# Loads of a decode kernel: from two half-loads on SyncE's and GpSimd's queues to whole loads on SyncE's

## The chip, the cores and the metric

The kernel runs on one core of one Trainium2 chip. The metric is the time of one execution on the device, in microseconds (us), lower being better; the median of three runs is given. The profile is of one execution and gives, beside that execution's time, the span: from the first to the last instruction of the program on the core.

## The reference

One token goes through an attention block with a cache and through a gated feed-forward block; the two results are mixed by a gate.

```python
# x: [1, 1, 512] bf16; 32 query heads, 8 key/value heads, head size 128, window W = 4096
g = sigmoid((x * gate_w).sum(-1))
# A: attention over the last W positions of the cache
q = (x @ wq)                              # wq [512, 4096]
k, v = k_cache[:, :, Sk - W:, :], v_cache[:, :, Sk - W:, :]   # each head of 8 serves 4 query heads
p = softmax(q . k * 128 ** -0.5)
a = (p . v).reshape(1, 1, 4096) @ wo      # wo [4096, 512]
# B: gated feed-forward
h = sigmoid(x @ w_gate) * (x @ w_up)      # w_gate, w_up [512, 1792]
b = h @ w_down                            # w_down [1792, 512]
out = g * a + (1 - g) * b
```

All weights and the two windows of the cache are read once from HBM: wq 4.2 MB, keys 8.4 MB, w_gate 1.8 MB, w_up 1.8 MB, values 8.4 MB, wo 4.2 MB, w_down 1.8 MB, 30.7 MB in all.

## The kernel before, in words

**Tiles and buffers.** The keys come in four tiles kn[a], each with a pair of heads on alternate partitions (even partitions the first head, odd ones the second), 128 partitions by 16 KB; the values in four tiles vv[a] of the same shape. Both kinds take their buffers from the pool blk, which has four: vv[a] goes where kn[a] was, and may be loaded when kn[a] has been read. wq_sb and wo_sb share the one buffer of the pool big (32 KB a partition). wg_sb, wu_sb and wd_sb (w_gate, w_up, w_down) take the three buffers of w14, one each. wx_sb is a small tile with a part of w_up, loaded in four pieces.

**Loads.** Every large load is written as two dma_start calls, one for the even partitions on SyncE's queue and one for the odd ones on GpSimd's (the loop over `queues`; load_pair, L109 to L113, does it for keys and values). The written order on either queue is wq, kn[0..3], wg, wu, (wx on SyncE alone,) vv[0..3], wo in two halves, wd in four pieces of 8, 3, 2 and 1 of its 14 rows a partition (WD_SPLIT). x and gate_w (xr, L76 and L77) are loaded first of all by GpSimd. At the end of the loads SyncE has an empty instruction that waits for the last sixteen of them (L155).

**Order.** Between instructions the framework's planner sets the semaphores. It also orders the instructions of an engine, by when it expects them to be ready, unless the engine is held to the written order by manual_schedule. SyncE and GpSimd are held so from L74 on, TensorE, VectorE and ScalarE from L192 on; the instructions of these three that are written ahead of L192 (x transposed by tiny matmuls, the gate g, the constants) are placed by the planner. GpSimd builds the constants (identity matrices, ones, zeroed qbig, a permutation) between its wq load and its key loads.

**Compute, in the order written.** (1) q: for each of eight blocks of 512 columns, four matmuls against wq_sb (L215), a copy by ScalarE, a transpose by VectorE for every two blocks (L220); then qbig is filled (L231). (2) Scores: for each kn[a], two transposes of 128 by 2048 on VectorE (L203) and 16 matmuls (L242). These transposes are the readers that kn[a] waits for before vv[a] may be loaded. (3) The gate branch glu(0) on wg_sb (L258), maximum, exponentials and sums of the softmax, their transpose eT. (4) pv: for each vv[a] 16 matmuls (L314). (5) The up branch glu(1) on wu_sb and wx_sb (L258, L255). (6) o: the sums of pv are brought into the shape of wo (L331, L333, L335, L337, L339); h is formed and transposed (L343, L348). (7) The output: 64 matmuls against wo_sb, then 28 against wd_sb, into one accumulator a_ps (L305); copies of its two halves (L356, L357), and the store.

Of the kernel before, what the change touches and what calls it, by code (L numbers as in the profile page):

```python
# [12 lines left out]
BF16 = mybir.dt.bfloat16  # L13
F32 = mybir.dt.float32
# [3 lines left out]
def kernel(  # L18
# [14 lines left out]
    nc = tc.nc  # L33

    P = 128
    D = A_x.shape[-1]
    DC = D // P
# [5 lines left out]
    W = min(4096, max(256, Sk // 4))  # L43
    KB = W // P
    SBASE = Sk - W
    F = B_w_gate.shape[1]
    NJ = F // P
    N_OUT = A_wo.shape[1]
    NC_O = HQ * DH // P
    FQ = F // 4  # L50
# [4 lines left out]
    HP = Hkv // 2  # L55
    R2 = 2 * REP
    NP = 2 * KB
    BIG = 1e30
    WD_SPLIT = (0, 8, 11, 13, 14)
    QUEUES = {mybir.EngineType.SP, mybir.EngineType.Pool}  # L60
    ORDERED = QUEUES | {mybir.EngineType.PE, mybir.EngineType.DVE, mybir.EngineType.Activation}

    const = ctx.enter_context(tc.tile_pool(name="const", bufs=1))
    big = ctx.enter_context(tc.tile_pool(name="big", bufs=1))
    blk = ctx.enter_context(tc.tile_pool(name="blk", bufs=4))
    w14 = ctx.enter_context(tc.tile_pool(name="w14", bufs=3))
# [4 lines left out]
    ps_m = ctx.enter_context(tc.tile_pool(name="ps_m", bufs=2, space=bass.MemoryType.PSUM))  # L71


    ctx.enter_context(tc.manual_schedule(engines=QUEUES))  # L74
    xr = const.tile([1, 2, D], BF16, name="xr")
    nc.gpsimd.dma_start(xr[:, 0, :], A_x[0, :, :])  # L76
    nc.gpsimd.dma_start(xr[:, 1, :], gate_w.rearrange("(o n) -> o n", o=1))  # L77

    dq = nc.sync
    queues = (dq, nc.gpsimd)  # L80
    loads = []
    wq_sb = big.tile([P, DC, HQ * DH], BF16, name="wq_sb", tag="big")
    wq_v = A_wq.rearrange("(p c) n -> p c n", c=DC)

    for y, queue in enumerate(queues):
        queue.dma_start(wq_sb[y:P:2], wq_v[y:P:2])  # L86


    identf = const.tile([P, P], F32, name="identf")
# [8 lines left out]
    permT = const.tile([P, P], BF16, name="permT")  # L98
    nc.gpsimd.tensor_copy(permT[:].rearrange("p (k j) -> p k j", j=4),  # L99
                          ident[:].rearrange("p (j k) -> p k j", j=4))  # L100

    other = const.tile([2, HQ * 4 // R2, 2, REP], BF16, name="other")
    nc.vector.tensor_scalar(other[:], ident[0:2, 0:2].rearrange("p (o y u) -> p o y u", o=1, u=1)  # L103
                            .to_broadcast([2, HQ * 4 // R2, 2, REP]), BIG, -BIG, op0=ALU.mult, op1=ALU.add)
    selI = const.tile([P, 32], F32, name="selI")
    nc.vector.tensor_reduce(selI[:], identf[:].rearrange("p (x r) -> p r x", x=4), axis=AX.X, op=ALU.add)


    def load_pair(t, cache, a, n0=0, n1=NP):  # L109
        for y, queue in enumerate(queues):  # L110
            loads.append(queue.dma_start(t[y:P:2, n0:n1, :].rearrange("p n d -> p (n d)"),  # L111
                                         cache[0, 2 * a + y, SBASE:SBASE + W, :].rearrange("(x n) d -> x n d", n=NP)
                                         [:, n0:n1, :].rearrange("x n d -> x (n d)")))  # L113

    kn = []
    for a in range(HP):
        kn.append(blk.tile([P, NP, P], BF16, name="kn", tag="blk"))
        load_pair(kn[a], A_k_cache, a)

    wg_sb = w14.tile([P, DC, F], BF16, name="wg_sb", tag="w14")  # L120
    wg_v = B_w_gate.rearrange("(p c) f -> p c f", c=DC)
    for y, queue in enumerate(queues):
        queue.dma_start(wg_sb[y:P:2], wg_v[y:P:2])
    wu_sb = w14.tile([P, DC, F], BF16, name="wu_sb", tag="w14")

    FX = 3 * FQ
    LM = DC * F - FX
    for y, queue in enumerate(queues):
        queue.dma_start(wu_sb[:].rearrange("p c f -> p (c f)")[y:P:2, 0:LM],
                        B_w_up.rearrange("(p c) f -> p (c f)", c=DC)[y:P:2, 0:LM])  # L130
    wx_sb = const.tile([64, 2, FX], BF16, name="wx_sb")
    wx_v = B_w_up.rearrange("(h b j i c) f -> h b i j c f", h=2, b=2, j=4, i=8)[:, :, :, :, DC - 1, F - FX:F]
    for h in range(2):
        for b in range(2):
            dq.dma_start(wx_sb[32 * b:32 * b + 32, h, :], wx_v[h, b])

    vv = []
    for a in range(HP):
        vv.append(blk.tile([P, NP, P], BF16, name="vv", tag="blk"))
        load_pair(vv[a], A_v_cache, a)  # L140

    wo_sb = big.tile([P, NC_O, N_OUT], BF16, name="wo_sb", tag="big")
    wo_v = A_wo.rearrange("(p c) n -> p c n", c=NC_O)
    for c0 in (0, NC_O // 2):
        for y, queue in enumerate(queues):
            loads.append(queue.dma_start(wo_sb[y:P:2, c0:c0 + NC_O // 2, :], wo_v[y:P:2, c0:c0 + NC_O // 2, :]))

    wd_sb = w14.tile([P, NJ, N_OUT], BF16, name="wd_sb", tag="w14")
    wd_v = B_w_down.rearrange("(p j) n -> p j n", j=NJ)
    for j0, j1 in zip(WD_SPLIT[:-1], WD_SPLIT[1:]):  # L150
        for y, queue in enumerate(queues):
            loads.append(queue.dma_start(wd_sb[y:P:2, j0:j1, :], wd_v[y:P:2, j0:j1, :]))  # L152


    seen = dq.nop()  # L155
    for load in loads[-16:]:
        tc.add_manual_dep(seen.ins, load.ins.name,
                          mybir.DependencyInfo(mybir.DependencyClass.Sync, mybir.DependencyReason.DATA), reason="loads ended")


    xt_ps = ps_m.tile([P, DC], F32, name="xt_ps", tag="m")
# [29 lines left out]

    ctx.enter_context(tc.manual_schedule(engines=ORDERED))  # L192

# [195 lines left out]
```

## Time and profile before

| | |
|---|---|
| median of 3 runs (lowest to highest) | 83.87 us (83.86 to 85.43) |
| profiled execution: time, span | 83.87 us, 82.1 us |
| granted TensorE clock, mean | 0.938 |
| busy: TensorE, VectorE, GpSimd, ScalarE | 54.1, 37.7, 13.5, 10.9 us |
| SyncE's transfer queue (q1): packets, MB | 1520, 15.51 |
| GpSimd's transfer queue (q0): packets, MB | 1312, 15.17 |
| first q matmul waiting for wq ends its wait | 16.31 us |
| vv[0] issued on SyncE, vv[3] issued on SyncE | 30.8, 43.96 us |

Times inside the profile are counted from the start of the span. A line of the timeline gives start and length in us, the engine, the line of the kernel, the operation and the tiles (written<-read), and in square brackets how long the engine was idle before and who ended that. PE is TensorE, DVE VectorE, ACT ScalarE, POOL GpSimd, SP SyncE; a q behind the name means the engine's sequencer, which issues transfers. In the slices' rows the span is cut into 40 equal parts; a digit is the busy share in tenths, and for DMA it is the mean share of the core's 16 transfer engines.

### The profile page before, as it was taken

Reading aid. Unit: us, or ns where it says so; the run is one execution under the profiler, and the core shown is the slowest. Engines: PE = TensorE matmul, PEld = TensorE weight load, DVE = VectorE, ACT = ScalarE, POOL = GpSimd, SP = SyncE. Lnnn points to the kernel's source line nnn. Section 1 sums busy time; section 2 is a strip of 40 time slices with the busy share of each in tenths; the row PEclk is TensorE's granted clock in tenths of the full one; section 3 lists DMA queues with packets and bytes.
Section 4 is the critical chain, followed back from the end, with each engine's and each line's share of the span. In section 5 each row is a group of like instructions: output and inputs, shape, how many; then the busy total and the mean of one; then the engine's idle time right before and its main releaser. Section 6 shows DMA issues by size and latency. Waiting matters only on the chain.

```text
span 82.1 us, 832 instructions
## 1 busy us (share of the span) xinstructions
PE 54.1 (66%) x314; PEld 24.2 (29%) x314; DVE 37.7 (46%) x48; ACT 10.9 (13%) x20; POOL 13.5 (16%) x29
## 2 busy tenths in 40 slices
PE   0000272099994199998888730079999989978970
PEld 0000240033441034433333210023353424446840
DVE  0000740000975999999999634994020000019520
ACT  6000000014465300000000229000000000200010
POOL 4999500000000002020204802010000000000000
PEclk9999999999999759999999999555799999999999
DMA  1989999899999999999999999999999999993000
GB/s 32 367 367 392 455 431 511 359 415 447 431 407 447 431 431 415 422 432 445 408 408 444 422 417 447 423 423 439 415 431 439 387 451 435 417 368 145 0 0 1
DMA packets 2836, 30.71 MB, mean 374 GB/s; under 512 B 641, under 2 KB 706, under 8 KB 1042
## 3 DMA queue, kind: packets, MB, share of 16 engines
q1 hardware_dynamic: 1520, 15.51, 45.3%
q0 software_dynamic: 1312, 15.17, 43.5%
q8 instruction: 2, 0.03, 0.2%
q10 hardware_dynamic: 2, 0.00, 0.0%
HBM read 30.67 MB, written 0.00 MB: 373 GB/s over the span
## 4 chain that ended last, share of the span: by engine, by line
DMA 58%; PE 14%; DVE 13%; POOL 7%; issue 5%; DVEq 0%; POOLq 0%
DMA kn<-in_A_k_cache_dram 29%; DMA vv<-in_A_v_cache_dram 29%; DVE kT L203 12%; PE a_ps L305 6%; PE pv_ps L314 4%; POOL qbig L97 2%; PE o_ps L331 1%; POOL kn L111 1%; POOL xr L76 1%; PE gu_ps L258 1%; POOL wq_sb L86 1%; PE gu_ps L255 1%; DVE res L356 0%; POOL permT L99 0%; POOL xr L77 0%
## 5 line engine op out<-in xcount | busy, mean ns | idle before, releaser
L314 PE MATMUL pv_ps<-vv,eT 128*32 128x512 bf16 x64 | 16.7, 420 | 5.5 <-DMA vv<-in_A_v_cache_dram 5.5
L242 PE MATMUL S_ps<-kT,qbig 128*128 128x512 bf16 x64 | 16.1, 401 | 4.1 <-DVE qbig L231 2.8
L203 DVE STREAM_TRANSPOSE kT<-kn 128x2048 f32<-128x2048 f32 x8 | 17.8, 2277 | 0.0
L215 PE MATMUL q_ps<-wq_sb,xT 128*128 128x512 bf16 x32 | 9.3, 462 | 3.4 <-DMA wq_sb<-in_A_wq_dram 3.4
L314 PEld LDWEIGHTS <-eT 128*32 128x32 bf16 x64 | 6.4, 105 | 14.9 <-DVE sge L294 5.1
L242 PEld LDWEIGHTS <-qbig 128*128 128x128 bf16 x64 | 6.4, 102 | 13.8 <-issue 4.4
L111 POOL DMA_DIRECT2D vv<-in_A_v_cache_dram x4 | 2.1, 536 | 33.3 <-DVE kT L203 33.3
L220 DVE STREAM_TRANSPOSE qtT<-q_sb 128x512 f32<-128x512 f32 x4 | 2.8, 702 | 9.6 <-ACT q_sb L217 9.6
L215 PEld LDWEIGHTS <-xT 128*128 128x128 bf16 x32 | 3.6, 113 | 9.5 <-issue 7.2
L333 DVE TENSOR_TENSOR oT<-o_ps,rb 128x32 bf16<-128x32 f32 x1 | 0.2, 191 | 12.6 <-PE o_ps L331 12.6
L217 ACT CAST q_sb<-q_ps 128x512 bf16<-128x512 f32 x8 | 4.7, 585 | 9.7 <-PE q_ps L215 9.7
L163 PE MATMUL xt_ps<-ident,xr 1*128 1x1 bf16 x4 | 0.3, 171 | 8.3 <-DMA xr<-in_A_x_dram 8.3
L168 DVE COPY xp<-xr 1x64 bf16<-1x64 bf16 x2 | 0.3, 200 | 8.3 <-DMA xr<-in_A_x_dram 8.3
L305 PE MATMUL a_ps<-wo_sb,oY 128*1 128x256 bf16 x64 | 3.7, 272 | 0.3 <-DVE oY L339 0.3
L152 POOL DMA_DIRECT2D wd_sb<-in_B_w_down_dram x4 | 2.2, 544 | 7.6 <-DMA vv<-in_A_v_cache_dram 7.6
L197 PE MATMUL S_ps<-ident,other 2*128 2x512 bf16 x4 | 2.0, 611 | 1.9 <-DVE other L103 1.9
L286 DVE STREAM_TRANSPOSE eT<-e_sb 128x1024 bf16<-128x1024 bf16 x2 | 2.4, 1224 | 1.9 <-ACT e_sb L284 1.9
L305 PEld LDWEIGHTS <-oY 128*1 128x1 bf16 x64 | 2.7, 84 | 1.7 <-DVE oY L339 1.1
L324 ACT COPY pv_sb<-pv_ps 128x512 f32<-128x512 f32 x1 | 0.6, 585 | 19.9 <-PE pv_ps L314 19.9
L269 ACT ACTIVATE sge<-gu_ps 128x448 f32<-128x448 f32 x1 | 0.5, 543 | 19.0 <-PE gu_ps L258 19.0
L296 DVE RECIPROCAL sg<-sge 128x448 f32<-128x448 f32 x1 | 3.0, 2953 | 0.0
L264 DVE TENSOR_REDUCE pm<-S_ps 128x1 f32<-128x1024 f32 x2 | 2.4, 1204 | 0.9 <-PE S_ps L242 0.9
(70 smaller groups left out, 38.3 us busy)
## 6 DMA issues: line engine op xcount, KB each, us to landing
kn<-in_A_k_cache_dram SPq DMA_DIRECT2D x4, 1024.0 KB, 24.4
kn<-in_A_k_cache_dram POOLq DMA_DIRECT2D x4, 1024.0 KB, 21.5
vv<-in_A_v_cache_dram SPq DMA_DIRECT2D x4, 1024.0 KB, 23.5
vv<-in_A_v_cache_dram POOLq DMA_DIRECT2D x4, 1024.0 KB, 19.6
wq_sb<-in_A_wq_dram SPq DMA_DIRECT2D x1, 2048.0 KB
wq_sb<-in_A_wq_dram POOLq DMA_DIRECT2D x1, 2048.0 KB, 13.9
wo_sb<-in_A_wo_dram SPq DMA_DIRECT2D x2, 1024.0 KB
wo_sb<-in_A_wo_dram POOLq DMA_DIRECT2D x2, 1024.0 KB, 25.9
```

The costliest lines, as they stand in the source:

```text
L111: loads.append(queue.dma_start(t[y:P:2, n0:n1, :].rearrange("p n d -> p (n d)"), cache[0, 2 * a + y, SBASE:SBASE + W, :].rearrange("(x n) ...
L152: loads.append(queue.dma_start(wd_sb[y:P:2, j0:j1, :], wd_v[y:P:2, j0:j1, :]))
L203: nc.vector.transpose(t[:].bitcast(F32), kn[a][:, v * KB:(v + 1) * KB, :] .rearrange("p n d -> p (n d)").bitcast(F32))
L215: nc.tensor.matmul(q_ps[:], lhsT=xT[:, c:c + 1].to_broadcast([P, P]), rhs=wq_sb[:, c, ks], start=(c == 0), stop=(c == DC - 1))
L217: nc.scalar.copy(q_sb[:, ks], q_ps[:])
L220: nc.vector.transpose(qtT[:].bitcast(F32)[:, kq], q_sb[:].bitcast(F32)[:, kq])
L242: nc.tensor.matmul(S_ps[v][:, hb, :], lhsT=q_st[:, a, dhi, :, t], rhs=k_v[:, hb * 16:(hb + 1) * 16, dhi, :, t], start=False, stop=(a == HP ...
L264: nc.vector.tensor_reduce(pm2[:, v:v + 1], S_ps[v][:].rearrange("p a b -> p (a b)"), axis=AX.X, op=ALU.max)
L286: nc.vector.transpose(eT[:, :, v * KB:(v + 1) * KB, :].rearrange("p a n r -> p n a r"), e_sb[:, v, :].rearrange("p (n a r) -> p n a r", a= ...
L296: nc.vector.reciprocal(sg[:], sge[:])
L305: nc.tensor.matmul(a_ps[32 * i:32 * i + 1, i, 0:HN], lhsT=lhsT, rhs=rhs[:, i * HN:(i + 1) * HN], start=start, stop=stop)
L314: nc.tensor.matmul(pv_ps[32 * a:32 * a + 32, :, :], lhsT=eT[:, a, 4 * m:4 * m + 4, :].rearrange("p n r -> p (n r)"), rhs=vv[a][:, 4 * m:4 ...
```

## The change

SyncE takes every large load but wq whole, all 128 partitions in one dma_start, written in the same order as before. Only wq keeps two loads, even partitions on SyncE and odd ones on ScalarE. GpSimd keeps x and gate_w. All load instructions now stand at the top of the kernel, ahead of the constants. The set ORDERED no longer has SyncE and GpSimd in it, and the early manual_schedule for these two is gone, so that the planner orders them throughout. The empty instruction at the end of the loads is gone. Four writes of zero to a one-element tile on VectorE are new.

```diff
-    QUEUES = {mybir.EngineType.SP, mybir.EngineType.Pool}
-    ORDERED = QUEUES | {mybir.EngineType.PE, mybir.EngineType.DVE, mybir.EngineType.Activation}
+    ORDERED = {mybir.EngineType.PE, mybir.EngineType.DVE, mybir.EngineType.Activation}
...
-    ctx.enter_context(tc.manual_schedule(engines=QUEUES))
     xr = const.tile([1, 2, D], BF16, name="xr")
     nc.gpsimd.dma_start(xr[:, 0, :], A_x[0, :, :])
     nc.gpsimd.dma_start(xr[:, 1, :], gate_w.rearrange("(o n) -> o n", o=1))
 
     dq = nc.sync
-    queues = (dq, nc.gpsimd)
-    loads = []
...
-    for y, queue in enumerate(queues):
+    for y, queue in enumerate((dq, nc.scalar)):
         queue.dma_start(wq_sb[y:P:2], wq_v[y:P:2])
+
+    def load_pair(t, cache, a, n0=0, n1=NP):
+        dq.dma_start(t[:, n0:n1, :].rearrange("p n d -> p (n d)"),
+                     cache[0, 2 * a:2 * a + 2, SBASE:SBASE + W, :]
+                     .rearrange("y (x n) d -> x y n d", n=NP)[:, :, n0:n1, :].rearrange("x y n d -> x y (n d)"))
...
+    dq.dma_start(wg_sb[:], B_w_gate.rearrange("(p c) f -> p c f", c=DC))
...
+    for c0 in (0, NC_O // 2):
+        dq.dma_start(wo_sb[:, c0:c0 + NC_O // 2, :], wo_v[:, c0:c0 + NC_O // 2, :])
...
+    for j0, j1 in zip(WD_SPLIT[:-1], WD_SPLIT[1:]):
+        dq.dma_start(wd_sb[:, j0:j1, :], wd_v[:, j0:j1, :])
...
+    spare = const.tile([1, 1], F32, name="spare")
+    for _ in range(4):
+        nc.vector.memset(spare[:], 0.0)
...
-    def load_pair(t, cache, a, n0=0, n1=NP):
-        for y, queue in enumerate(queues):
-            loads.append(queue.dma_start(t[y:P:2, n0:n1, :].rearrange("p n d -> p (n d)"),
-                                         cache[0, 2 * a + y, SBASE:SBASE + W, :].rearrange("(x n) d -> x n d", n=NP)
-                                         [:, n0:n1, :].rearrange("x n d -> x (n d)")))
...
-    seen = dq.nop()
-    for load in loads[-16:]:
-        tc.add_manual_dep(seen.ins, load.ins.name,
-                          mybir.DependencyInfo(mybir.DependencyClass.Sync, mybir.DependencyReason.DATA), reason="loads ended")
```

## The prediction

> **What bounds the kernel now.** I read the page's slices first, then the chain that ended last, then SyncE's waits, then the transfers in two narrow windows. Slices of the span (one is 2.05 us; digits are tenths):
>
> ```profile
> DMA  1989999899999999999999999999999999993000
> GB/s 32 367 367 392 455 431 511 359 415 447 431 407 447 431 431 415 422 432 445 408 408 444 422 417 447 423 423 439 415 431 439 387 451 435 417 368 145 0 0 1
> ```
>
> From slice 1 to slice 35 the 16 transfer engines are full, at about 0.425 MB/us (the page: 30.71 MB). No compute engine is full for so long, so the sum of the bytes is the floor, and two things are open to a change: the rate, and what is left to do after the last byte. The chain's last pieces (start, length, what):
>
> ```profile
> 43.96 23.66 DMA vv<-in_A_v_cache_dram
> 67.62 0.04 issue
> 67.67 2.97 PE pv_ps L314 x13
> ...
> 72.35 1.02 PE o_ps L331 x8
> ...
> 74.35 5.23 PE a_ps L305 x92
> 79.58 0.40 DVE res L356
> ```
>
> The fourth value block, vv[3], lands at 67.62, and everything after it is serial: pv, o, oT, oX, oY, then 92 output matmuls. From that landing to the end of the span is 82.10 - 67.62 = **14.48 us**. SyncE's own waits show when the last load of all is in:
>
> ```profile
> SPq L155 <- DMA wd_sb<-in_B_w_down_dram: 16.7, 4, 15.9
> ```
>
> SyncE's last load issue starts at 58.73 and takes 0.47; 59.20 + 16.7 = **75.9**. So wd lands while the output matmuls already run, and does not hold them up.
>
> **Bytes and rate.** The same bytes move after the change, so I need the rate of one queue alone. Just before GpSimd's bulk begins, SyncE's queue (q1) is alone but for 16 tiny packets; this is the transfer view of 3.8 to 7.4 us:
>
> ```profile
> DMA packets 64, 1.57 MB, mean 437 GB/s; under 512 B 16, under 2 KB 16, under 8 KB 16
> q1 hardware_dynamic: 48, 1.57, 102.0%
> q0 software_dynamic: 16, 0.00, 0.3%
> ```
>
> One queue with rows of 32 KB fills the engines as well as two (437 against mostly 410 to 450 in the middle slices). I take an unchanged rate. The bounds: 0.437 throughout would end the loads 30.7 / 0.425 - 30.7 / 0.437 = 2.0 us earlier; the first full slice, 367 while the queue starts up, would if it lasted end them 11 us later. The window is nearer to a steady stream than the start-up slice, so I give the rate +/- 1 us.
>
> [...]
>
> **Issue costs.** GpSimd loses 17 load issues (1 wq, 4 kn, wg, wu, 4 vv, 2 wo, 4 wd) of about 0.54 (the 536 ns of its vv row): 9.2 us on an engine that is idle after 10 us. At the end this is worth nothing; at the start its setup moves up by the 0.56 of the wq issue. SyncE issues 21 loads before and 21 after, now of 128 rows; if an issue goes by instruction it stays at 0.60, if by rows it doubles to 1.2. The first seven then take 4 to 8 us, while the first 4.2 MB alone occupy the engines for 4.2 / 0.425 = 9.9 us: hidden either way, and at most 0.6 us if that cover were gone. ScalarE gets one issue of about 0.53 (SyncE's wq row) ahead of or behind its table load of 1.28 at 0.73; its next instruction waits 9.6 us for z_ps, which hides both. Four one-element memsets on VectorE, near 0.1 each by the other tiny rows, lie in its 8.3 us wait for x. The dropped nop waits only for loads: nothing.
>
> **wq earlier.** GpSimd's half is issued at 2.37, lands at 16.3 and starts the q matmuls. From SyncE and ScalarE at once, both halves share the engines from about 2.7 (first bytes at 2.05, some 0.6 lost in the slow first slice): 2.7 + 9.9 = 12.6, so 12.5 to 14. The q matmuls, the first key transposes and so the release of the first kn buffer (SyncE issues vv[0] at 30.8) come some 2 to 3.5 us earlier. At 30.8 the queue still holds 16.3 MB less about 12 MB, that is 10 us of work, so an earlier vv issue fills no hole: zero at the end.
>
> **The order of SyncE's loads.** This decides the time. Before, both queues are in the set that manual_schedule holds to the written order: kn, wg, wu, wx, vv, wo, wd. After, ORDERED names PE, DVE and Activation alone, and SyncE's loads are left to the planner. The trace shows how that planner treats an engine not held by hand; VectorE's timeline before the hand-ordered part:
>
> ```profile
> 8.32 0.33 DVE L168 COPY xp<-xr 1x64 bf16<-1x64 bf16 x2 [8.32 <-DMA xr<-in_A_x_dram]
> 8.94 0.68 DVE L180 TENSOR_TENSOR gpr<-xr 1x512 f32<-1x512 bf16 x1 [0.29 <-DMA xr<-in_gate_w_dram]
> 9.65 0.67 DVE L181 TENSOR_REDUCE gsum<-gpr 1x1 f32<-1x512 f32 x1
> 10.25 0.35 DVE L106 TENSOR_REDUCE selI<-identf 128x32 f32<-128x128 f32 x1
> 10.53 0.20 DVE L103 TENSOR_SCALAR other<-ident 2x128 bf16<-2x128 bf16 x1
> ```
>
> L103 and L106 are written first, and L168, L180 and L181, expected ready sooner, are put ahead of them. The same rule on SyncE: vv[a] shares its buffer with kn[a] and must wait for two key transposes; wo shares with wq and is free after the last q matmul (25.6), ahead of the first release of a kn buffer (30.8); wd has a buffer of its own and is free at once. So I expect **kn, wg, wu, wx, wd, wo, vv**: the value cache last.
>
> **The forecast.** SyncE waits in between (a load also waits for an older one whose semaphore it takes over: the trace has wx waiting for wq and kn), but by the time wu is in, near 40, wx and most of wd are queued and wo and vv follow; no hole. The last load is then vv[3]. With large rows at the end the thin last stretch goes (slice 36 still moves 145 GB/s in rows of 1 to 3 KB): 75.9 becomes about 75.4, between 74.4 and 76.4 with the rate's bounds. From there the whole 14.48 is left, since glu(1), o and the output matmuls stand behind pv on TensorE and need it. 75.4 + 14.5 = 89.9 of span. The profiled execution took 83.87 with a span of 82.1, and its time is also the median, so I add 1.77: **91.7 us**, 9% slower; 90.5 to 93.0 for this case alone. Put as a difference: the same chain starts 75.4 - 67.6 = 7.8 us later.
>
> **Rivals.** First, and on the other side: **the written order holds** on SyncE, because the planner blocks at the first load that waits for a buffer. One queue then lands vv[3] after 24.6 MB, near 2.7 + 24.6 / 0.425 = 60.6, some 7 us sooner than its later half does now; vv leaves the chain. wo is in by about 71, wd at 75.9 as now, and after the last wd piece there are only two matmuls (0.4), then from the copy of the result to the end 82.1 - 79.58 = 2.5. Span 78.8, time 80.6, 4% faster; 79.4 to 82.0. For it: two queues drift apart today, the last vv issued at 43.96 on SyncE landing at 67.6 and GpSimd's at about 44.2 + 19.6 = 63.8. Against it: the VectorE rows. The point that decides is whether vv[0] stands ahead of wd and wo on SyncE.
>
> Second: **only part of the order moves**. If wd alone passes vv, vv[3] lands near 2.7 + 26.5 / 0.425 = 65, wo ends the loads at 75.9 and leaves 32 + 28 output matmuls (60 x 5.23 / 92 = 3.4) and the 2.5: span 81.8, time 83.6, no change. The written order with a rate 3 to 4% lower ends there too. Against it: wo's release precedes vv's by 5 us in the trace.
>
> Third: **one queue is slower**. At the 392 of slice 3 the written order ends 6 us later than the first rival, 86.6, and the forecast's order at 97. Against it: the lone-queue window above.
>
> **How the numbers follow.** Forecast's order 0.58; written order at full rate 0.24; the mixed cases 0.14; a slower queue in the written order 0.04. What a measurement of this kernel can tell from no change is about 2%, 82.2 to 85.5. Faster by more is the first rival, 0.24; within it the mixed cases, 0.14; slower the forecast and the slow queue, 0.62. The time is the forecast's, 91.7; its own range is 90.5 to 93.0. To hold eight in ten the range must reach over to the first rival: 80.0 to 93.4.
>
> **What would show it.** In the changed profile: the order of SyncE's issues (wd and wo between wx and vv); the chain ending in vv, pv, o, a_ps with vv landing at 75 to 76 and the transfer row empty for the last seven slices; the slices before it still at 415 to 450 GB/s; one hardware queue with nearly all bytes; the first q matmul at 12.5 to 14.5. I am wrong if vv is issued before wo, if the last load is wd, or if the middle slices fall under 410.

## The result, and the profile after

The changed kernel runs in 80.8 us (80.77 and 80.88) against 83.86 to 83.89 before; the ratio is **0.964, 95% interval 0.961 to 0.967**, so it is faster by 3.6%. (Some executions of either kernel are some 2% longer; their times are left out here and below, which is why the plain median of the four runs, 81.66, is not the one used.) The forecast was 91.7; the first rival, the written order kept on SyncE, had 80.6, with a span of 78.8.

The slices of the changed kernel (span 79.2, one slice 1.98 us):

```profile
DMA  0999797999999999999999999999999999999700
GB/s 0 265 530 481 315 530 331 447 414 414 455 439 414 406 455 447 393 435 404 430 429 435 431 406 422 439 447 397 431 439 422 430 431 431 422 402 387 283 30 1
```

The transfers are as full as before (mean rate from 42 to 72 us 424 GB/s, before 425) and end at about the same time (76.2 us, before 76.1); the empty stretch behind them is shorter. SyncE's timeline (start, length from the first issue to the last of the group, and the load; line numbers are those of the changed kernel):

```profile
1.35 2.54 SPq L86 DMA_DIRECT2D kn<-in_A_k_cache_dram  x4
3.93 0.59 SPq L96 DMA_DIRECT2D wg_sb<-in_B_w_gate_dram  x1
4.57 0.43 SPq L101 DMA_DIRECT2D wu_sb<-in_B_w_up_dram  x1
13.80 9.87 SPq L107 DMA_DIRECT2D wx_sb<-in_B_w_up_dram  x4
31.86 13.69 SPq L86 DMA_DIRECT2D vv<-in_A_v_cache_dram  x4
45.64 1.02 SPq L117 DMA_DIRECT2D wo_sb<-in_A_wo_dram  x2
46.71 5.72 SPq L122 DMA_DIRECT2D wd_sb<-in_B_w_down_dram  x4
```

The values stand where they are written, ahead of wo and wd. The end of the chain, and from the view of the tile vv the time from issue to landing:

```profile
47.65 28.19 DMA wd_sb<-in_B_w_down_dram
75.85 0.04 issue
75.89 0.66 PE a_ps L292 x6
76.55 0.40 DVE res L343
```

```profile
DMA to landing us min/median/max: 15.3/15.8/16.9
```

The last value load is issued at 45.0, so vv[3] is in by 45.0 + 16.9 = 61.9, where it was 67.62 before. No pv matmul waits for it any more; the softmax does the holding (pv begins at 52.7, after the transpose eT). The chain now ends in the third of wd's four pieces, in at 75.85, with six output matmuls left to do, and 79.2 - 75.85 = 3.35 us follow it, in place of 14.48 after vv[3]. The fourth piece lands while these matmuls run. Its rows in the views of the issues (size, us to landing), the kernel before first, with SyncE's half:

```profile
wd_sb<-in_B_w_down_dram SPq DMA_DIRECT2D x1, 64.0 KB, 17.3
```

```profile
wd_sb<-in_B_w_down_dram SPq DMA_DIRECT2D x1, 128.0 KB, 24.1
```

Issued at 58.73 and at 52.10, it is in at about 76 in both, 76.08 and 76.19 by the landings in the traces (the prediction had read 75.9 from SyncE's waits). So the 2.9 us of span come from the end alone: the last byte lands when it did, but the work that stood behind vv[3] is now done while the last loads are still running.

### The profile page after: what moved, and what is told of

It is laid out like the page before. It is cut to its first block, busy times and chain, and to the rows that moved or that the text cites. A ratio compares the mean times of both kernels' runs of the same rounds, so it can differ in the third digit from the quotient of the medians.

```text
span 79.2 us, 800 instructions
## 1 busy us (share of the span) xinstructions
PE 52.6 (66%) x314; PEld 23.7 (30%) x314; DVE 37.9 (48%) x52; ACT 10.8 (14%) x20; POOL 4.4 (6%) x12
## 4 chain that ended last, share of the span: by engine, by line
DMA 50%; DVE 17%; PE 16%; issue 10%; SPq 3%; ACT 1%; POOL 1%; DVEq 0%; POOLq 0%
DMA wd_sb<-in_B_w_down_dram 36%; DMA xr<-in_gate_w_dram 14%; PE q_ps L202 12%; DVE kT L190 11%; PE S_ps L184 2%; DVE qbig L218 2%; SPq L117 1%; SPq L122 1%; DVE qtT L207 1%; DVE gpr L167 1%; DVE gsum L168 1%; PE a_ps L292 1%; ACT q_sb L204 1%; SPq L86 1%; POOL xr L74 1%
## 5 line engine op out<-in xcount | busy, mean ns | idle before, releaser
L301 PE MATMUL pv_ps<-vv,eT 128*32 128x512 bf16 x64 | 14.2, 412 | 2.8 <-DVE eT L273 2.8
L301 PEld LDWEIGHTS <-eT 128*32 128x32 bf16 x64 | 5.8, 103 | 10.3 <-DVE eT L273 2.9
L155 DVE COPY xp<-xr 1x64 bf16<-1x64 bf16 x2 | 0.3, 202 | 8.3 <-DMA xr<-in_A_x_dram 8.3
L292 PE MATMUL a_ps<-wd_sb,hT 128*1 128x256 bf16 x28 | 2.1, 271 | 0.6 <-DMA wd_sb<-in_B_w_down_dram 0.6
(64 smaller groups left out, 31.9 us busy)
```

Of the source, the lines that this page charges most:

```text
L292: nc.tensor.matmul(a_ps[32 * i:32 * i + 1, i, 0:HN], lhsT=lhsT, rhs=rhs[:, i * HN:(i + 1) * HN], start=start, stop=stop)
L301: nc.tensor.matmul(pv_ps[32 * a:32 * a + 32, :, :], lhsT=eT[:, a, 4 * m:4 * m + 4, :].rearrange("p n r -> p (n r)"), rhs=vv[a][:, 4 * m:4 ...
```

## The experiments

Two questions: why was the order not the forecast's, and why is one queue faster than two? For the second, three theories. **A**: in the kernel before, wx's small rows let GpSimd's queue overtake SyncE's on half of the transfer engines, so that SyncE's half of vv[3] was late. **B**: a second queue costs time as such. **C**: half-loads of 64 rows do.

**e1: the forecast's order, by hand.**

```diff
-    vv = []
-    for a in range(HP):
-        vv.append(blk.tile([P, NP, P], BF16, name="vv", tag="blk"))
-        load_pair(vv[a], A_v_cache, a)
-
     wo_sb = big.tile([P, NC_O, N_OUT], BF16, name="wo_sb", tag="big")
...
         dq.dma_start(wd_sb[:, j0:j1, :], wd_v[:, j0:j1, :])
 
+    vv = []
+    for a in range(HP):
+        vv.append(blk.tile([P, NP, P], BF16, name="vv", tag="blk"))
+        load_pair(vv[a], A_v_cache, a)
+
```

> The changed kernel with the loads of wo and wd written ahead of those of the values, so that SyncE issues kn, wg, wu, wx, wo, wd, vv: the order that the prediction expected. If the prediction's arithmetic was right and only its order wrong, vv[3] lands last, near 75.4, the whole 14.5 us from there to the end is left, and the time is 91 to 92.5. If the tail is shorter when all weights are in already (the output matmuls or the up branch move under the loads), the time is 86 to 89. If the order of the loads matters little, 81 to 83.

Measured: 92.7 us, span 91.0. The chain's end:

```profile
52.36 24.05 DMA vv<-in_A_v_cache_dram
76.41 0.04 issue
76.45 2.96 PE pv_ps L301 x13
...
88.35 0.40 DVE res L343
```

vv[3] lands at 76.41 and 91.0 - 76.41 = 14.6 us follow. The tail was right within 0.1; the landing came 1.0 later than the 75.4 of the sum, and the time 0.2 above the 91 to 92.5 given for this case. The transfer engines did not finish together here either, with large rows at the end: in the trace vv[3] is in at 74.3 to 74.7 on seven of the sixteen and at 75.9 to 76.4 on the other nine. But for that 1.0, the forecast's arithmetic stands with the order that it assumed.

**e8: values written ahead of wg, wu and wx**, SyncE still left to the planner.

```diff
+    vv = []
+    for a in range(HP):
+        vv.append(blk.tile([P, NP, P], BF16, name="vv", tag="blk"))
+        load_pair(vv[a], A_v_cache, a)
+
     wg_sb = w14.tile([P, DC, F], BF16, name="wg_sb", tag="w14")
...
-    vv = []
-    for a in range(HP):
-        vv.append(blk.tile([P, NP, P], BF16, name="vv", tag="blk"))
-        load_pair(vv[a], A_v_cache, a)
-
     wo_sb = big.tile([P, NC_O, N_OUT], BF16, name="wo_sb", tag="big")
```

> The changed kernel with the loads of the values written right behind those of the keys, ahead of wg, wu and wx, and SyncE still left to the planner. In the trace of the changed kernel vv[0] waits until 31.9 for its buffer, and wg and wu wait for nothing. If the planner put SyncE's loads in order of readiness, as the prediction held, wg, wu and wx would be issued ahead of vv, near 4 us, and the time would be 80.5 to 82. If it keeps SyncE's written order, SyncE stands before vv[0] until about 32 with wg not issued, the transfers run dry for some 1 us near 32, wg lands only near 57, and since glu(0) and the softmax stand ahead of pv on TensorE, pv begins near 66 and the time is 90 to 94.

Measured in one run: 92.9 us. Of SyncE's timeline, and the first gate matmul:

```profile
1.37 2.94 SPq L86 DMA_DIRECT2D kn<-in_A_k_cache_dram  x4
31.54 13.69 SPq L86 DMA_DIRECT2D vv<-in_A_v_cache_dram  x4
45.28 0.59 SPq L101 DMA_DIRECT2D wg_sb<-in_B_w_gate_dram  x1
```

```profile
59.61 1.69 PE L245 MATMUL gu_ps<-wg_sb,xT 128*32 128x448 bf16 x16 [12.98 <-DMA wg_sb<-in_B_w_gate_dram]
```

wg could have been issued at 4.3 us, behind the last key load, and SyncE stands for 27 us before a buffer instead. No load passed vv[0] while it waited: wg was issued at 45.28, behind all four value loads.

**e9: a wait for data on SyncE.**

The constants that GpSimd builds (identf to permT) stand ahead of the key loads here, and SyncE copies the last of them.

```diff
+    identf = const.tile([P, P], F32, name="identf")
+    make_identity(nc, identf[:])
...
+    cpy = const.tile([P, P], BF16, name="cpy")
+    dq.dma_start(cpy[:], permT[:])
     kn = []
...
-    identf = const.tile([P, P], F32, name="identf")
-    make_identity(nc, identf[:])
...
```

> The changed kernel with the constants written ahead of the key loads and one more small SyncE transfer there: a copy of permT, which GpSimd writes by about 5.5 us, into a tile that nobody reads. This is a wait for data, as VectorE's L103 had in the trace of before, where the planner put later instructions ahead of it. If it does so on SyncE, kn is issued at 1.4 as in the changed kernel. If it keeps SyncE's written order, the first kn issue stands behind the copy, at 5.5 to 6.5; the 4.2 MB of wq cover that, and the time stays at 80.6 to 81.6.

Measured in one run: 80.9 us. SyncE's timeline:

```profile
0.73 0.56 SPq L82 DMA_DIRECT2D wq_sb<-in_A_wq_dram  x1
5.52 0.51 SPq L103 DMA_DIRECT2D cpy<-permT  x1
6.07 4.41 SPq L86 DMA_DIRECT2D kn<-in_A_k_cache_dram  x4
```

The key loads wait behind the copy, to 6.07. In these kernels the planner kept SyncE's transfers in the written order past a wait for a buffer (e8) and past a wait for data (e9); what VectorE's rows showed did not carry over. Why it treats the two engines differently no run shows.

**e2: the kernel before without wx**, still two queues.

```diff
-        queue.dma_start(wu_sb[:].rearrange("p c f -> p (c f)")[y:P:2, 0:LM],
-                        B_w_up.rearrange("(p c) f -> p (c f)", c=DC)[y:P:2, 0:LM])
-    wx_sb = const.tile([64, 2, FX], BF16, name="wx_sb")
...
+        queue.dma_start(wu_sb[y:P:2], B_w_up.rearrange("(p c) f -> p c f", c=DC)[y:P:2])
...
-                if w == 1 and c == DC - 1 and j >= 1:
...
```

> The kernel before, still with every large load as two halves on SyncE's and GpSimd's queues, but w_up loaded whole and no wx (its six matmuls of 64 rows become three of 128). Theory A, small rows: the trace of before has wx's rows of 2.7 KB spread over 38 to 49 us, while GpSimd's queue moves 2.62 MB and SyncE's 1.59 MB from 40 to 50; each engine takes the two queues' rows in turn, wx falls on half of the engines, and there GpSimd's 16 KB rows overtake, so that SyncE's half of vv[3] lands some 8 us late. Then without wx vv[3] lands at 61 to 65, the chain ends in wd, and the time is 80.3 to 81.5. Theory B, two queues as such, or GpSimd's transfers, cost the 3 us: the time stays at 83.5 to 84.5. Theory C, half-loads (64 rows) cost it: 83.5 to 84.5 as well.

Measured: 81.2 to 81.6 us, ratio to the kernel before 0.970 (0.966 to 0.973). The trace is of an execution of 84.3 us with a granted TensorE clock of 0.827, so only the transfers are read from it. The transfer view of 35 to 45 us (queue: packets, MB, share), the kernel before first, then e2:

```profile
q0 software_dynamic: 233, 2.74, 64.7%
q1 hardware_dynamic: 224, 1.55, 37.1%
```

```profile
q1 hardware_dynamic: 168, 2.16, 50.9%
q0 software_dynamic: 176, 2.08, 49.1%
```

With wx in its queue, SyncE's side falls 1.2 MB behind in these 10 us; without it the two are level. The trace gives the landings engine by engine. Before, SyncE's half of vv[3] lands on eight engines at 56.8 to 58.5 and on the other eight at 67.2 to 67.6, ten us apart within one load; in e2 all sixteen are in by 59.4. So about five sixths of the gain (3.0% of 3.6%) come with wx leaving the two-queue kernel: A. But the time lies at the upper end of the range that A gave, and two of A's signs failed, vv[3] in by 61 to 65 and a chain that ends in wd:

```profile
44.29 21.25 DMA vv<-in_A_v_cache_dram
65.54 0.04 issue
```

vv still ends it: GpSimd's half of vv[3] is in only at 65.54, 6 us after SyncE's, whose queue has a head start (GpSimd builds constants until 6 us). SyncE's queue has moved 6.52 MB after 30 us where GpSimd's has moved 5.25, and 13.08 against 11.52 after 60: the lead is there early and stays.

**e3: both halves from SyncE.**

```diff
-    queues = (dq, nc.gpsimd)
+    queues = (dq, dq)
```

> The kernel before with both halves of every large load issued by SyncE, even partitions first; nothing else is moved and wx stays. A (small rows beside a second queue) and B (a second queue as such): 80.3 to 81.5, vv[3] landing at 60 to 63. C (half-loads as such): 83.5 to 84.5, with fewer GB/s in the middle slices. More loads wait for an older one whose semaphore they take over; if that lets the queue run dry, a hole shows between 34 and 45 us and the time is up to 3 us longer.

Measured: 80.7 to 80.9 us, ratio 0.963 (0.960 to 0.966): all of the change's gain from this one line, with wx and the half-loads in place; vv[3] is in at 61.7. From 42 to 72 us:

```profile
DMA packets 1034, 12.73 MB, mean 424 GB/s; under 512 B 204, under 2 KB 204, under 8 KB 215
q1 hardware_dynamic: 1033, 12.72, 100.1%
```

C falls: half-loads move at the 424 GB/s that the changed kernel's whole loads have in the same window. No hole shows either. Nor did a second queue lower the rate; the kernel before, in the same window:

```profile
DMA packets 1168, 12.76 MB, mean 425 GB/s; under 512 B 246, under 2 KB 246, under 8 KB 370
```

A and B both allow e3's time; e2 tells them apart, together with e4 below.

**e5: two of wx's four pieces on GpSimd's queue**, and once more for a second profile.

```diff
-            dq.dma_start(wx_sb[32 * b:32 * b + 32, h, :], wx_v[h, b])
+            queues[b].dma_start(wx_sb[32 * b:32 * b + 32, h, :], wx_v[h, b])
```

> The kernel before with wx kept, two of its four pieces on GpSimd's queue in place of SyncE's. A: the small rows now stand in both queues, neither overtakes by more than half as much, the later half of vv[3] lands at 62 to 66, and the time is 80.3 to 82. B and C: 83.5 to 84.5.

> The same kernel as the one with wx on both queues, for a profile in which TensorE's clock is not low. Its time was 0.8 to 1 us under the kernel before, where theory A gave 2 to 3.5. If A holds in part, GpSimd's queue still moves more than SyncE's from 35 to 45 us and the later half of vv[3] lands at 66 to 67, about 1 us earlier than before; if vv[3] lands by 65 and the time is still 82.8, something other than the landing of vv holds the end.

Measured: 82.8, 83.0 and 84.0 us, ratio 0.992 (0.984 to 1.000), not told from no change; A's 80.3 to 82 failed. The execution profiled with them took 116.8 us and is not used. The second set gave 84.2 and 85.9 us, beside 85.4 and 85.5 for the kernel before. Its trace is of the 85.9, and only the transfers are read from it:

```profile
q0 software_dynamic: 252, 2.13, 51.3%
q1 hardware_dynamic: 243, 2.11, 50.8%
```

These are 35 to 45 us again: the totals are level now, where GpSimd's was expected to be larger, and still vv[3] lands as late as in the kernel before, not at 66 to 67. Its last half is GpSimd's this time:

```profile
43.90 24.09 DMA vv<-in_A_v_cache_dram
67.98 0.04 issue
```

In the trace it comes in on eight engines at 62.9 to 63.3, on the other eight at 66.4 to 68.0. SyncE's half comes in on eight at 54.7 to 56.3 and on the other eight at 60.5 to 60.8, where in e2, without wx, fifteen of the sixteen had it at 57.5 to 57.9: some 3 us sooner on the one half, some 3 us later on the other. It seems that wx's small rows held back GpSimd's queue here as they had SyncE's in the kernel before, each on the engines that carried them; that the pieces of the two queues fell on different engines is inferred from these landings and was not tried by itself. A's account of the mechanism is left standing, but what it made of sharing wx between the queues is not.

**e4 and e7: the changed kernel without wx, and with two thirds of it.**

```diff
-    dq.dma_start(wu_sb[:].rearrange("p c f -> p (c f)")[:, 0:LM],
-                 B_w_up.rearrange("(p c) f -> p (c f)", c=DC)[:, 0:LM])
-    wx_sb = const.tile([64, 2, FX], BF16, name="wx_sb")
...
-            dq.dma_start(wx_sb[32 * b:32 * b + 32, h, :], wx_v[h, b])
+    dq.dma_start(wu_sb[:], B_w_up.rearrange("(p c) f -> p c f", c=DC))
...
-                if w == 1 and c == DC - 1 and j >= 1:
...
```

```diff
-    FX = 3 * FQ
+    FX = 2 * FQ
...
-                if w == 1 and c == DC - 1 and j >= 1:
+                if w == 1 and c == DC - 1 and j >= 2:
...
```

> The changed kernel with w_up loaded whole and no wx. In one queue no second queue can overtake, so by theory A wx costs or gains only what it does to the balance of the engines at the end of the loads: the time is within 0.6 of the changed kernel, 80.3 to 81.4. If small rows cost time by themselves, wherever they stand, it is 79 to 80.

> The changed kernel with wx two thirds as large (the last two of four column blocks in place of three). If the end of the loads is set by the half of the engines that carry wx, which are some 1.6 us later than most others, the last load is in 0.2 to 0.3 earlier and the time is 80.4 to 80.7; if by one engine without wx that is as late, 80.8 to 81.

Measured: e4 81.8 to 82.0 (ratio to before 0.975, 0.973 to 0.977), e7 81.0 to 82.1 (0.969, 0.961 to 0.976). Both guesses were off: in one queue wx does not cost, it gains 1.0 us. e4's last output matmuls start later than the 75.89 of the changed kernel:

```profile
76.62 0.66 PE a_ps L279 x6
```

In e4's trace the third of wd's four pieces, which these matmuls wait for, lands on fourteen engines by 75.3 and on the other two only at 76.5 to 76.6. In the changed kernel's trace each of wx's four pieces lands on eight of the sixteen engines (the first at 40.7 to 41.0), so the 84 KB of a piece lie there and not on the others; that this relieved the late ones is the likely reason, but which engines those are was not shown. e7's intervals do not tell it from the changed kernel.

With e2 this also speaks against B. Without wx, two queues take 81.2 to 81.6 us and one queue 81.8 to 82.0; with wx they take 83.9 and 80.8. (e4 has the rest of the change too, which with wx in place adds nothing to e3's one line.) So two queues were slower than one only with wx in one of them. The two kernels without wx end differently, e2 with vv's later half and e4 with the two late engines, so a small cost of the second queue's lead is not excluded.

**e6: x and gate_w from ScalarE.**

```diff
-    nc.gpsimd.dma_start(xr[:, 0, :], A_x[0, :, :])
-    nc.gpsimd.dma_start(xr[:, 1, :], gate_w.rearrange("(o n) -> o n", o=1))
+    nc.scalar.dma_start(xr[:, 0, :], A_x[0, :, :])
+    nc.scalar.dma_start(xr[:, 1, :], gate_w.rearrange("(o n) -> o n", o=1))
```

> The changed kernel with x and gate_w loaded by ScalarE ahead of its half of wq, in place of GpSimd. In the changed kernel's trace gate_w lands at 13.2 and the q matmuls start at 17.2, though wq is in at 13.8: the prediction had 12.5 to 14.5. If x and gate_w wait behind the large rows, they now land by 4 to 5 us and q starts at 13.5 to 15. By the theory that the transfers alone set the end, this moves the time by less than 0.4 (80.4 to 81.2); if the start of q matters, it is 78 to 79.5.

Measured: 80.7 to 80.9 us, ratio 0.963 (0.961 to 0.964). q now starts at 14.55, 2.6 us earlier, and the last output matmuls at 75.78:

```profile
14.55 8.47 PE q_ps L202 x32
...
75.74 0.04 issue
75.78 0.66 PE a_ps L292 x6
```

The start of q is worth nothing here, where the transfers never run dry (423 GB/s from 12 to 31 us in the changed kernel). e3 and e6 reach the changed kernel's time and do not beat it.

## Why the prediction was wrong

**The step that failed is the order of SyncE's loads.** The prediction read five rows of VectorE, saw later instructions put ahead of earlier ones, and held that the planner would treat SyncE's loads so too. SyncE issued vv[0] at 31.9, wo at 45.6 and wd from 46.7 instead, the written order; vv[3] landed at 61.9 and not at 75.4, and the time was 80.8 and not 91.7. The rows were right for VectorE (the compiled order after the change still has L155, L167 and L168 of the new numbering ahead of L145 and L142), but no row of before showed SyncE outside a hand-held order, so it was an extension from one engine to another. What is said ahead of the prediction, that the planner orders an engine by when it expects its instructions to be ready, fits these rows of VectorE and not SyncE's loads. The case got 0.58 and was the likeliest; e8 and e9 show that it holds on SyncE neither for buffers nor for data. The range of 80.0 to 93.4 holds 80.8 only because it reached over to the first rival; the forecast itself had the kernel slower. The point that was named as deciding, whether vv[0] stands ahead of wd and wo, did decide.

**The sums around it held.** The tail of 14.5 after vv[3] measured 14.6 in e1. The first rival's terms came out nearly as written: vv[3] at 60.6 against 61.9, the last load at 75.9 against 76.2, from there to the end of the span 2.9 against 3.0 (the chain runs through the piece before the last, at 75.85 with six output matmuls left and not two), time 80.6 against 80.8. Mis-sized in the forecast's own sum was the last landing, 75.4 against 76.4 in e1: large rows at the end did not shorten the thin stretch.

**The rate of one queue.** Read from 3.6 us of the trace as unchanged, it held: 12.7 MB from 42 to 72 us in one queue, 424 GB/s, with rows of 16 and 8 KB for nearly all of these bytes. Two queues moved 425 in the same window before.

**Issue costs** went by instruction: four key loads of 128 rows in 2.54 us, 0.6 each, where four of 64 rows took 2.55 before. The second rival (only part of the order moves) and the third (a slower queue) did not happen.

**wq earlier** was right for the load and wrong for q: both halves were in by 13.8, but q started at 17.2 and not at 12.5 to 14.5. x and gate_w took longer to land, 7.0 each before, and what stands ahead of q on TensorE needs gate_w:

```profile
xr<-in_A_x_dram POOLq DMA_DIRECT2D x1, 1.0 KB, 8.3
xr<-in_gate_w_dram POOLq DMA_DIRECT2D x1, 1.0 KB, 11.3
```

```profile
1.85 11.33 DMA xr<-in_gate_w_dram
...
13.20 0.69 DVE gpr L167
...
15.88 1.30 PE S_ps L184 x3
17.18 9.56 PE q_ps L202 x32
```

The prediction moved wq alone and gave no later landing to x and gate_w, which now stand beside two queues of 32 KB rows. So the first key buffer came free 1.1 us later than before (vv[0] issued at 31.9, before at 30.8), and not 2 to 3.5 earlier. As e6 shows, this is off the path.

**What the prediction did not see** is why two queues were slow. It noted that the two halves of vv drift apart (67.6 against 63.8; the trace has GpSimd's at 64.6) and used it for the rival, without asking what makes them drift. Had it asked, the answer, wx, would not have changed the order question.

## What to carry to other kernels

Both kernels kept the transfers full (425 and 424 GB/s from 42 to 72 us), and what was left to gain was in the work behind the last needed byte, 14.48 us behind vv[3] before and 3.35 behind wd's third piece after: put the loads in the order of need, so that each lands whole before the next. A load split over two queues landed with its later half, 6 us behind the first in e2, and in the kernel before a small-row load in one of them let the other run ahead on eight engines, where SyncE's half of vv[3] came in ten us after the other eight. One queue was faster than two only with that load in place. How the planner ordered one engine did not tell how it ordered another; where the order decides the time, hold it by hand, or give both orders equal weight.

## What the runs showed of the hardware

Where wx stood beside GpSimd's half-loads, a transfer engine took one row of each queue in turn, though the rows differed sixfold in length. In the trace of before, the four pieces of wx (four rows of 2.7 KB on each of eight engines) land 2.7 to 2.9 us after one another: four times a row of 16 KB from GpSimd's queue (0.612) and one of 2.7 KB (0.107) is 2.88. In the changed kernel they are 0.4 apart: four times 0.107 is 0.43. One row at a time is what fits the 2.88. That a load of 1 KB took 8.3 and 11.3 us to land beside two queues of 32 KB rows, and 7.0 before, may come of the same turns; no run tried that by itself.
